# A fused attention and max-out kernel on one core: the written-out order of its work is replaced, and its dummy products get wider

## The chip, the core and the metric

The kernel runs on one NeuronCore of a Trainium2 chip. Five engines take their instructions from queues of their own, each strictly in the order in which they were written: TensorE (PE in the profile; its weight loads are listed as PEld), VectorE (DVE), ScalarE (ACT), GpSimd (POOL) and SyncE (SP), which here only issues DMAs. An instruction waits at the head of its queue until the semaphores that it needs are up, and everything behind it waits with it. The metric is the device time of one execution in microseconds (us).

## The reference, cut to what matters

Four batches of eight heads, 768 positions, head size 64. Three of the heads see all earlier keys; the other five see the first four keys and a window of 64. The concatenated heads are the input of a max-out layer.

```
scores = q @ k.T / 8                                # per head, 768 x 768
mask   = causal                                     # is_retrieval heads (0, 2, 6)
mask   = causal & (key < 4 | query - key < 64)      # the others
a      = softmax(scores masked)
x      = concat over heads of a @ v                 # 3072 tokens x 512
g      = maximum(x @ w1, x @ w2)                    # 512 -> 1024, twice
out    = g @ w_out                                  # 1024 -> 512
```

## The kernel before, in words

The kernel computes the layer as relu(x (w1 - w2)) w_out + x (w2 w_out): so it needs the difference w12 = w1 - w2 (line 1139, "sub"), and once the product w2o = w2 w_out on PE (lines 1156 and 1183).

Work is cut in eight halves: four batches, 384 query rows each. The order of the halves is batch 0 first half, batch 1 first half, batch 0 second half, batch 1 second half, then the two halves of batch 2 and of batch 3. A half goes through these steps. q, k and v land as f32 in one of three staging slots (tile ld). They are cast to bf16 (qb, vb; lines 366 and 368 are the helper that copies, on ACT and on DVE or POOL). PE turns q and k (line 645; in the last three halves a DMA does), a copy takes them out of PSUM (qk). PE makes the scores (915), ACT takes their exponential (930, tile at), DVE multiplies with the mask (955), PE forms the weighted sums (980), DVE divides by the row sums (997 and 1007, "norms") into x. x is turned (1103 on PE for the first three halves, by DMA for the others) and the layer follows one half later: "up" (1206, 32 products of 384 columns), relu on ACT (1231) or DVE (1233), "down" (1263, 36 products of 512 columns), a copy to ot, a store (1291).

Batch 0's first half has a detour for v: it is loaded in the layout that DMA moves best, and PE spreads it to the right rows (688).

The weights come through the same three slots. w2 comes in two column halves of 1 MB, w1 likewise, w_out in four pieces of 0.5 MB. Each w2 half is cast (w2b, four casts of 1024 columns in all), turned by PE in four groups of eight (1156), taken out of PSUM as w2t. Each w_out piece is cast to wob. The four pieces of w_out feed four groups of products for w2o (1183): group c needs w2t c and wob c. Slots are freed by casts: w_out's first piece may be issued when the q of batch 0's first half is cast, the second when q and k are, the third when k is, the fourth when v is; batch 1's q and k go into the slot of w_out and wait for the casts of wob.

What stands in front of all this: the order is not found by a scheduler at run time. The kernel collects 1097 operations, and `Order.run` (line 137 on) emits them in the order of a table of tokens, PLAN, and a short one, LAST. A token is the operation's number, a letter for the engine that does it (p PE, a ACT, v DVE, g POOL, s SP) and the PSUM banks that it takes; so the table sets three things: the order on each engine's queue, which engine does a cast or copy that several could do, and the bank. A token x is a dummy product on PE (line 353): `warmer`, a tile of zeros, times itself, into a bank that is free, its result never read. The dummies fill places where PE would have nothing to do in the first 24 us.

## Time and profile before

| what | value |
|---|---|
| median of 3 runs (lowest, highest) | 176.43 us (176.25, 176.6) |
| the profiled execution: first to last instruction | 175.4 us |
| PE busy | 168.5 us, 96% |
| ACT busy | 126.3 us, 72% |
| DVE busy | 122.0 us, 70% |
| POOL busy | 34.2 us, 19% |
| granted TensorE clock, mean | 0.997 |
| DMA | 36.14 MB, mean 206 GB/s; 334 to 389 GB/s in the page's slices from 4.4 to 26 us |

The profiled execution's own span is 175.4 us; the median of the runs lies 1.03 us above it. Times in the profile are us from the first instruction of that execution. A row of the timeline gives start, length, engine, line, operation, what it writes and reads, how many equal instructions were merged, and in brackets how long the engine had been idle before and what released it. The records of PE products overlap, since a product's record runs until its result has left the array: a row with 8 products of 512 columns is 1.89 us long, and the next product may start some 0.16 us before its end.

### The profile page before, as it was taken

The numbers are of one execution on the slowest core, as the hardware profiler recorded it, in microseconds if no ns is written. First come the engines' busy times: TensorE is split into PE (matmuls) and PEld (weight loads), VectorE is DVE, ScalarE is ACT, GpSimd is POOL, SyncE is SP. The second block draws the span as 40 slices with busy tenths as digits, with TensorE's granted clock in tenths as the row PEclk, the third lists the DMA queues.
The fourth block names the chain that finished last, engine by engine and source line by source line (L and its number), as shares of the span: only waits on it lengthen the run. The fifth ranks groups of instructions, "written<-read, shape, count | busy, mean of one in ns | idle before, by whom it ended". The sixth has DMA issues, their size and how long they took to land.

```text
span 175.4 us, 4945 instructions
## 1 busy us (share of the span) xinstructions
PE 168.5 (96%) x1795; PEld 105.5 (60%) x1816; DVE 122.0 (70%) x331; ACT 126.3 (72%) x280; POOL 34.2 (19%) x78
## 2 busy tenths in 40 slices
PE   7999799999999999999999999999999999999993
PEld 7976575655665666666656545764565566545542
DVE  5579899686999997887858666666884168941211
ACT  3499807998999998999997669795858598405200
POOL 5732132422414613040200240000012000000000
PEclk9999999999999999999999999999999999999998
DMA  4999999999899999992597993339999334453004
GB/s 129 334 371 389 387 382 333 214 312 298 201 248 258 281 300 211 234 283 71 152 190 192 238 225 76 71 69 237 213 242 176 67 87 153 154 153 122 0 7 179
DMA packets 77661, 36.14 MB, mean 206 GB/s; under 512 B 59202, under 2 KB 72514, under 8 KB 77634
## 3 DMA queue, kind: packets, MB, share of 16 engines
q1 hardware_dynamic: 77488, 35.73, 78.4%
q8 instruction: 15, 0.25, 0.6%
q14 instruction: 12, 0.10, 0.2%
q10 hardware_dynamic: 146, 0.07, 0.1%
HBM read 25.17 MB, written 6.29 MB: 179 GB/s over the span
## 4 chain that ended last, share of the span: by engine, by line
PE 85%; DMA 6%; POOL 3%; issue 2%; DVE 2%; POOLq 0%; ACT 0%; DVEq 0%; SPq 0%; ACTq 0%
PE ps L1263 36%; PE ps L1206 24%; PE ps L915 9%; PE ps L980 8%; DMA ld<-in_moe_w_dram 6%; PE ps L645 3%; PE ps L1183 3%; POOL tab L1605 1%; PE ps L1103 1%; DVE at L955 1%; PE ps L353 1%; DVE x L1007 0%; POOL tab L1619 0%; POOL g L705 0%; POOLq L1670 0%
## 5 line engine op out<-in xcount | busy, mean ns | idle before, releaser
L930 ACT ACTIVATE at<-ps 128x512 bf16<-128x512 f32 (+2 forms) x134 | 64.1, 573 | 6.4 <-PE ps L915 6.2
L1206 PE MATMUL ps<-xt,w 128*128 128x384 bf16 x256 | 45.8, 326 | 0.0
L1263 PE MATMUL ps<-wob,g 128*128 128x512 bf16 (+2 forms) x192 | 44.7, 370 | 0.4
L955 DVE TENSOR_TENSOR at<-at,tab 128x1024 bf16<-128x1024 bf16 (+5 forms) x56 | 29.9, 549 | 10.7 <-ACT at L930 10.3
L1206 PEld LDWEIGHTS <-w 128*128 128x128 bf16 x256 | 23.9, 98 | 16.0 <-issue 0.4
L1263 PEld LDWEIGHTS <-g 128*128 128x128 bf16 x200 | 18.0, 98 | 18.8 <-issue 0.2
L1231 ACT ACTIVATE g<-ps 128x384 bf16<-128x384 f32 x37 | 18.0, 502 | 11.1 <-PE ps L1206 10.0
L1233 DVE TENSOR_SCALAR g<-ps 128x384 bf16<-128x384 f32 x27 | 14.6, 550 | 15.8 <-PE ps L1206 15.7
L1263 PE MATMUL ps<-w2o,xt 128*128 128x512 bf16 (+2 forms) x90 | 23.5, 370 | 0.5
L1007 DVE TENSOR_TENSOR x<-ps,rez 128x192 f32 x64 | 22.7, 355 | 1.6
L368 POOL CAST qb<-ld 128x384 bf16 (+1 forms) x28 | 13.2, 505 | 50.5 <-DMA ld<-in_q_dram 30.6
L366 ACT COPY ot<-ps 128x512 f32<-128x512 f32 (+1 forms) x18 | 10.4, 575 | 17.0 <-PE ps L1263 16.8
L980 PEld LDWEIGHTS <-at 128*128 128x128 bf16 x477 | 18.6, 97 | 6.3 <-DVE at L955 1.2
L980 PE MATMUL ps<-vb,at 128*128 128x65 bf16 x387 | 20.4, 193 | 0.4 <-DVE at L955 0.4
L915 PE MATMUL ps<-qk 64*128 64x128 bf16 (+1 forms) x330 | 18.4, 228 | 0.2
L915 PEld LDWEIGHTS <-qk 64*128 64x128 bf16 x330 | 12.2, 94 | 7.2 <-issue 4.7
L368 DVE COPY qk<-ps 128x384 bf16<-128x384 bf16 (+1 forms) x17 | 11.3, 693 | 3.9 <-PE ps L645 3.8
L1263 PEld LDWEIGHTS <-xt 128*128 128x128 bf16 x100 | 8.9, 97 | 8.5
L366 ACT CAST qb<-ld 128x384 bf16 (+1 forms) x31 | 11.8, 440 | 2.8 <-DMA ld<-in_q_dram 1.7
L353 PE MATMUL ps<-warmer 128*128 128x128 bf16 x133 | 12.1, 256 | 1.4 <-POOL warmer L1655 1.2
L353 PEld LDWEIGHTS <-warmer 128*128 128x128 bf16 x133 | 10.5, 118 | 1.7 <-POOL warmer L1655 1.2
L368 POOL CAST vb<-ld 128x192 bf16 x15 | 5.7, 406 | 24.6 <-DMA ld<-in_v_dram 24.5
(74 smaller groups left out, 161.4 us busy)
## 6 DMA issues: line engine op xcount, KB each, us to landing
ld<-in_v_dram SPq DMA_DIRECT2D x21, 256.0 KB, 5.0
ld<-in_moe_w_dram SPq DMA_DIRECT2D x4, 1024.0 KB, 11.8
out_dram<-ot SPq DMA_DIRECT2D x16, 256.0 KB, 3.4
ld<-in_q_dram SPq DMA_DIRECT2D x5, 768.0 KB, 7.3
ld<-in_k_dram SPq DMA_DIRECT2D x5, 768.0 KB, 8.4
ld<-in_k_dram SPq DMA_DIRECT2D x9, 256.0 KB, 4.5
ld<-in_q_dram SPq DMA_DIRECT2D x9, 256.0 KB, 4.9
ld<-in_moe_w_out_dram SPq DMA_DIRECT2D x4, 512.0 KB, 10.6
```

Source lines behind the costliest of these rows:

```text
L353: nc.tensor.matmul(banks[e][:, 0:128 * m].rearrange("p (m c) -> p m c", m=m), lhsT=warm, rhs=warm.unsqueeze(1).to_broadcast([128, m, 128]) ...
L366: nc.scalar.copy(out=out, in_=in_)
L368: eng[e].tensor_copy(out=out, in_=in_)
L915: nc.tensor.matmul(to.rearrange("p (i c) -> p i c", c=128), lhsT=lhsT, rhs=q_of(n, i, m)[rows], start=True, stop=True, skip_group_check=True,)
L930: nc.scalar.activation(out=at[:, bk, 0:w], in_=bank(("ps", b, hf, t), part=bk)[:, 0:w], func=ACT.Exp, scale=scale,)
L955: eng[e].tensor_tensor(out=at, in0=at, in1=tbl, op=ALU.mult)
L980: nc.tensor.matmul(po[:, hh, i - NT * hf, :], lhsT=ats[:, T["at", b, hf, t] % NAT, bk, e * 128:(e + 1) * 128], rhs=rhs, start=first, stop= ...
L1007: nc.vector.tensor_tensor(out=xs[:, HALVES.index((b, hf)) % NX, :, bass.ds(heads[2 * p + hh], 1), :], in0=po[:, hh, :, 0:D].unsqueeze(2), ...
L1206: nc.tensor.matmul(bank(key)[:, 0:HALF], lhsT=w[:, kc, fc * 128:(fc + 1) * 128], rhs=xts[:, HALVES.index((b, hf)) % NXT, :, kc, :], start= ...
L1231: nc.scalar.activation(out=g, in_=ph, func=ACT.Relu)
L1233: nc.vector.tensor_scalar_max(out=g, in0=ph, scalar1=0.0)
L1263: nc.tensor.matmul(bank(key)[:, cols], lhsT=lhsT, rhs=(w2o if kind == "x" else wob)[:, c, cols], start=(e == 0), stop=(e == len(steps) - 1),)
```

## The change

The two tables are replaced by new ones with the same 1097 operations; what each operation computes, and its buffers, are untouched. The numbers of operations by engine shift, since a few casts and copies are given to another engine: tokens for ACT go from 279 to 265, for DVE from 305 to 314, for POOL from 62 to 67. A new token y is a dummy product of 512 columns (the `dummy` function had that size as an argument already). There are 29 of these in place of 133 of 128 columns. As `run` loses no line and the table has two lines fewer, every line below it is numbered two lower in the changed kernel (1183 becomes 1181).

```diff
@@ -137,10 +137,10 @@ Order.run
         for token in plan.split():
-            if token[0] == "x":
+            if token[0] in "xy":
                 spot, _, times = token[1:].partition("*")
                 for _ in range(int(times or 1)):
-                    self.dummy(int(spot))
+                    self.dummy(int(spot), 4 if token[0] == "y" else 1)
                 continue
@@ -152,64 +152,62 @@
 PLAN = """
-0s x0*3 1s x0*5 2s x0*36 3s 66a 50v x0*3 28a 64v x0 48g x0 58a x0 68p0 26a 25g x1*2 52p1 56a 69v 44p2 x3 4s
...
+0s y0 1s y0 2s y0 y1*3 y2*3 3s y3*3 y4 56a 26v y4 50a 58v y4 64a 66v y5 28a 48v y5 8s 52p0 44p1 60p2 4s y3 45v
...
 LAST = """
-1082v 1085p 1083s 1077a 1086p 1078s 1089p5 1087v 1090p 1091p 1088s 1092a 1093a
+1082a 1083s 1084p6 1077v 1085p 1078s 1086p 1089p5 1087a 1090p 1091p 1088s 1092v 1093a
 """
```

Three places of the new order are shown. The names carry the program's buffer numbers: ld is the staging slot, w2b the cast of w2, w2t its turned form, wob the cast of w_out, vb the spread v, at the exponentials, rez the reciprocals of the row sums, x the attention's result.

SP, the first loads. Before, from batch 0's q to batch 1's k:

```order
L426 DMA ld_61<-in_q_dram 128x8x192
L426 DMA ld_61<-in_k_dram 128x8x192
L426 DMA ld_61<-in_v_dram 128x8x192
L531 DMA ld_61<-in_moe_w2_dram 128x4x512
L552 DMA ld_61<-in_moe_w_out_dram 128x2x512
L531 DMA ld_61<-in_moe_w2_dram 128x4x512
L552 DMA ld_61<-in_moe_w_out_dram 128x2x512 x2
L531 DMA ld_61<-in_moe_w1_dram 128x4x512
L552 DMA ld_61<-in_moe_w_out_dram 128x2x512
L531 DMA ld_61<-in_moe_w1_dram 128x4x512
L426 DMA ld_61<-in_q_dram 128x8x192
L426 DMA ld_61<-in_k_dram 128x8x192
```

and now:

```order
L424 DMA ld_61<-in_q_dram 128x8x192
L424 DMA ld_61<-in_k_dram 128x8x192
L424 DMA ld_61<-in_v_dram 128x8x192
L529 DMA ld_61<-in_moe_w2_dram 128x4x512 x2
L550 DMA ld_61<-in_moe_w_out_dram 128x2x512 x4
L529 DMA ld_61<-in_moe_w1_dram 128x4x512 x2
L424 DMA ld_61<-in_q_dram 128x8x192
L424 DMA ld_61<-in_k_dram 128x8x192
```

The second half of w2 goes ahead of all of w_out, and w1 behind all of it; the four pieces of w_out come in their own order.

ACT, from the last copy of v to the first products of the layer. Before:

```order
L366 CAST vb_143<-ps0_155 128x8x64
L930 ACTIVATE at_148<-ps4_159 128x512
L366 COPY w2t_140<-ps7_162 128x1024
L930 ACTIVATE at_148<-ps2_157 128x512
L366 CAST w2b_138<-ld_61 128x4x256
L930 ACTIVATE at_148<-ps3_158 128x512
L366 COPY w2t_140<-ps5_160 128x1024
L366 COPY w2t_140<-ps2_157 128x1024
L366 COPY xt_150<-ps2_157 128x1024
L366 COPY xt_150<-ps1_156 128x512
```

and now:

```order
L364 CAST w2b_138<-ld_61 128x4x256
L364 CAST vb_143<-ps2_157 128x8x64
L928 ACTIVATE at_148<-ps4_159 128x512
L928 ACTIVATE at_148<-ps5_160 128x512
L928 ACTIVATE at_148<-ps7_162 128x512
L364 CAST wob_142<-ld_61 128x1024
L364 COPY w2t_140<-ps0_155 128x1024
L364 CAST wob_142<-ld_61 128x1024
L364 COPY xt_150<-ps3_158 128x1024
L364 COPY xt_150<-ps6_161 128x512
```

Two casts of w_out (its second and third piece) stand in ACT's queue, two copies of w2t have left it. Of the four casts of w_out POOL had three and DVE one; now ACT has two, DVE one (the first piece) and POOL one (the last).

DVE, from the last cast of w2 to the first norms. Before:

```order
L368 COPY w2t_140<-ps5_160 128x1024
L997 RECIPROCAL rez_63<-ps1_156 128x6
L368 CAST w2b_138<-ld_61 128x4x256
L1007 ISA
L1007 TENSOR_TENSOR x_149<-ps1_156,rez_63 128x3x64
```

and now:

```order
L366 CAST w2b_138<-ld_61 128x4x256
L366 COPY w2t_140<-ps6_161 128x1024
L366 CAST wob_142<-ld_61 128x1024
L953 TENSOR_TENSOR at_148<-at_148,tab_60 128x1024
L366 COPY w2t_140<-ps1_156 128x1024
L366 COPY w2t_140<-ps3_158 128x1024
L953 TENSOR_TENSOR at_148<-at_148,tab_60 128x1024
L995 RECIPROCAL rez_63<-ps2_157 128x6
```

The norms of batch 0's first half, which began among the masks and casts, all stand behind them now, and the four subs behind the norms as before.

On PE the last dummies stood behind the last weighted sums of batch 0's first half (29 of 128 columns, ahead of the second group of products for w2o); now the last dummy stands ahead of the third turned group of w2, and from there on PE has real work alone. The layer's eight "up" of the first half now come in one row, ahead of the turning of batch 1's q, and two groups of "down" stand among the turnings.

More of the change, by code (lines that the diff above doesn't have):

```diff
@@ new lines @@
+144p 117p3 119p6 118a 155p 148p 121v 150p 120a 146p 151a 125v 211p2 19s 156a 209p0 213p3 129v 215p6 133v 18s
+222p4 216a 214a 220p7 223a 157v 181g 195a 226p6 197a 212v 183g 210a 224p3 159g 169a 227v 167g 221a 17s 163p4
+149a 187p2 225v 201p0 173p6 147v 218p7 20s 158a 160g 170a 198g 184v 182a 165p1 21s 229p 174v 168g 166a 196g 164v
+202a 175p3 425s 188a 189p5 203p6 176v 190a 244p10 240p42 177v 246a 179v 219p3 204v 171g 242a 172g 200v 241a 185g
+247p50 205v 245a 252p62 186a 191v 423s 230p 207v 180a 199v 254a 193v 161v 249a 208v 234p 243v 253a 248a 206v
@@ new lines @@
+294g 337v 433a 295g 334p2 339v 300g 443g 333a 330p7 335v 451g 438p3 314v 331a 316v 396p6 306v 326v 397p 439a
+398p 426s 380p14 372p05 440v 381a 305v 392p27 315v 399p 373a 233s 342p3 400v 393a 554s 446p1 374a 343v 349p0
+673s 320a 375v 382a 317v 325g 350p 307a 447v 581a 562g 676s 394a 571g 402v 384p25 493p34 401v 385a 377p17 453g
+561v 386a 327v 388p62 376v 675s 351p 390a 383v 395v 379a 565p5 448v 389a 344p2 378a 391v 352a 403p7 387v 454p6
+353s 410p1 455a 404p 405p 236s 415p 409p0 566a 416v 411p 572v 345p 551s 418v 495a 417v 671s 406v 346p 456v 553s
@@ new lines @@
+841s 776a 718p0 711a 615a 720p3 933s 719v 772a 358s 716p5 704v 769v 814a 929s 771a 781p 712p4 758v 842s 688v
+721v 607p7 713a 693g 833v 777v 927s 791p0 722p6 815s 938v 608p 952v 723a 782v 765v 835v 816s 773v 724p1 709v
+714p3 953v 725a 784v 488s 726p4 715a 821s 793p 785p6 794v 792p1 717v 797p 786p 931s 787p 736p3 928s 788v 783v
+930s 823v 790v 727p 789v 798v 799v 796v 728p 800v 825v 843v 845v 795v 609p 729v 801s 737p 610a 882p52 616s
+894p61 884a 885p04 896a 611s 902p72 738p 937g 886a 730s 945g 883a 944g 904a 731p1 826g 887a 942g 895a 732p 960g
@@ new lines @@
+959g 903a 897v 951a 898p05 939g 890p24 878p67 891a 733p 905v 879a 936v 892a 949v 941s 943v 868p2 880a 957v 893v
+958a 734v 849p6 900a 940s 888v 899a 881v 859p4 950a 857p7 955s 916p1 858a 918p 861p5 919v 850a 860v 947s 961a
+847p0 901v 862a 906p7 921v 855p6 920v 621s 956v 889v 907p 853p4 856v 735s 908v 851p5 910v 954s 854a 848a 917p1
+922p 739a 911p6 923v 912p 925v 863p4 946s 852a 913v 914v 924v 864p 948v 909v 965v 915v 1001p03 926s 997p51 1002a
+1007p76 869p 998a 1008a 962s 870p 999a 1009a 865p 1003a 740s 871a 1010p05 963s 866v 1022p71 1012a 1015p63
```

84 lines of the change are left out of this document (31 added, 53 removed).

## The prediction

> **What bounds the kernel now.** I read the head of the page and the chain of waits first, then PE's own waits.
>
> ```profile
> span 175.4 us, 4945 instructions
> PE 168.5 (96%) x1795; PEld 105.5 (60%) x1816; DVE 122.0 (70%) x331; ACT 126.3 (72%) x280; POOL 34.2 (19%) x78
> PE 85%; DMA 6%; POOL 3%; issue 2%; DVE 2%; POOLq 0%; ACT 0%; DVEq 0%; SPq 0%; ACTq 0%
> L353 PE MATMUL ps<-warmer 128*128 128x128 bf16 x133 | 12.1, 256 | 1.4 <-POOL warmer L1655 1.2 <-ACT at L930 0.2
> PE ps L1156 <- DVE w2b L368: 0.8, 1, 0.8
> PE ps L980 <- DVE at L955: 0.4, 2, 0.2
> ```
>
> PE is 85% of the chain. Its only named waits are 1.2 us before the first dummy and 1.4 us after it, all before 22 us. But 12.1 us of its busy time are dummies, so its free time is there. PE's timeline shows where:
>
> ```profile
> 13.76 2.10 PE L688 MATMUL ps<-xt,g 128*128 128x512 bf16 x8
> 16.65 0.78 PE L980 MATMUL ps<-vb,at 128*128 128x65 bf16 x20
> 17.44 1.25 PE L1183 MATMUL ps<-wob,w2t 128*128 128x512 bf16 x5
> 19.48 1.07 PE L1156 MATMUL ps<-tab,w2b 128*128 128x128 bf16 x16 [0.78 <-DVE w2b L368]
> 21.65 0.54 PE L980 MATMUL ps<-vb,at 128*128 128x65 bf16 x12 [0.15 <-DVE at L955]
> 22.13 1.78 PE L353 MATMUL ps<-warmer 128*128 128x128 bf16 x29
> 23.75 1.89 PE L1183 MATMUL ps<-wob,w2t 128*128 128x512 bf16 x7
> 30.25 2.76 PE L1206 MATMUL ps<-xt,w 128*128 128x384 bf16 x16
> 32.85 0.67 PE L645 MATMUL ps<-tab,qb 128*128 128x128 bf16 x9
> 36.24 0.62 PE L915 MATMUL ps<-qk 64*128 64x128 bf16 x15
> ```
>
> The reader is to see two places where PE lacks work after 19 us: it waits 0.78 us for the second half of w2, and at 22.13 it turns dummies for 1.62 us until w_out is there. From 23.75 on it goes from one real product to the next. So the span is: the time until PE has unbroken work, the work behind that, and some 3 us of tail. Only the first of these can move much. Later stretches show little that is idle:
>
> ```profile
> 35.00:60.00 25.00, 24.59 (x267) 15.10 (x268) 22.19 (x61) 23.59 (x56) 9.85 (x20) 1.00 1.03 266
> 60.00:95.00 35.00, 34.64 (x462) 22.25 (x467) 27.54 (x77) 33.14 (x75) 5.29 (x11) 1.00 0.87 208
> 95.00:160.00 65.00, 64.48 (x621) 36.83 (x628) 41.48 (x120) 43.28 (x97) 5.27 (x13) 1.00 0.69 150
> ```
>
> (columns: window, length, PE, PEld, DVE, ACT, POOL busy, clock, DMA share, GB/s.) PE is idle for 0.41, 0.36 and 0.52 us there. ACT is the second bound up to 95 us: 56.7 of 60 us busy.
>
> **The change part by part.** *The landings.* These set when PE has real work:
>
> ```profile
> 7.72 0.47 SPq L531 DMA_DIRECT2D ld<-in_moe_w_dram  x1
> 9.45 0.88 SPq L552 DMA_DIRECT2D ld<-in_moe_w_out_dram  x2
> 13.38 0.70 DVE L368 CAST w2b<-ld 128x1024 bf16<-128x1024 f32 x1 [0.42 <-DMA ld<-in_moe_w_dram]
> 16.04 1.04 POOL L368 CAST wob<-ld 128x1024 bf16<-128x1024 f32 x1 [3.82 <-DMA ld<-in_moe_w_out_dram]
> 18.73 0.69 DVE L368 CAST w2b<-ld 128x1024 bf16<-128x1024 f32 x1 [0.66 <-DMA ld<-in_moe_w_dram]
> 21.45 1.04 POOL L368 CAST wob<-ld 128x1024 bf16<-128x1024 f32 x1 [4.37 <-DMA ld<-in_moe_w_out_dram]
> 25.46 1.94 POOL L368 CAST wob<-ld 128x1024 bf16<-128x1024 f32 x1 [2.96 <-DMA ld<-in_moe_w_out_dram]
> ```
>
> Between 18.73 and 21.45 two pieces of w_out land (0.5 MB each), between 21.45 and 25.46 half of w1 and a piece: 2 and 3 units of 0.5 MB, so 1.35 us a unit. In the new order w2's second half (issued at 7.72 before) has one unit less ahead of it: 18.73 - 1.35 = 17.4. From below it is bounded by the place of the piece that stood there, 16.04; from above by no move, 18.73. Of the three I take 17.4, by the unit. The pieces of w_out follow: the first at 18.7 (as many bytes ahead of it as w2's half had), then 20.1, 21.4, 22.8; w1's halves at 25.5 and 28.2.
>
> *From there to the layer.* PE's last dummy ends near 17.3: before it stand v's spread (at 13.7, since the last cast of v still follows four exponentials on ACT, as it did at 13.76), two turned groups of w2 and two of the scores. The third turned group starts at 17.4 + 0.7 (the cast) = 18.1. What PE has to do from there to the end of the first half's "up" is counted from the rows. Before, from 19.48 to 36.24 it is 16.76 us; less the dummies (23.75 - 22.13 = 1.62) and the wait (0.15) it is 14.99. 24 turnings of q and k (9 of them take 0.67 - 0.16 = 0.51, so 1.36 in all) now come later: 13.63. Behind 18.1 now come also the 20 weighted sums of 16.65 (0.79 to the next row) and the first three groups for w2o (six products; eight take 1.89 - 0.16 in the row of 23.75, which lacks one, so 1.30): 15.72. So "up" would end at 33.8 if nothing waits; in the old order the same work is done at 36.24 - 1.36 = 34.9. That is a gain of 1.1.
>
> *What it costs in waits.* The new order hangs more on ACT and DVE here:
>
> ```profile
> 11.97 3.54 ACT L930 ACTIVATE at<-ps 128x512 bf16<-128x512 f32 x7
> 15.33 0.65 ACT L366 CAST vb<-ps 128x512 bf16<-128x512 f32 x1
> 20.16 1.92 ACT L366 COPY w2t<-ps 128x1024 bf16<-128x1024 bf16 x2
> 23.83 1.53 DVE L1007 TENSOR_TENSOR x<-ps,rez 128x192 f32 x4
> L1139 DVE TENSOR_TENSOR w<-ld x4: 1209/1213/2059, 25.3 to 29.5; 128x1024 bf16<-128x1024 f32 x4
> ```
>
> An exponential takes (15.33 - 11.97) / 7 = 0.48 on ACT, a copy of 1024 columns 0.95; so the next instruction starts some 0.1 before a record's end, and DVE's casts count 0.6. ACT: w2's cast from 17.4 to 18.35, v's copy 18.8, three exponentials 20.3, the second piece of w_out 21.3 (landed 20.1), w2t 22.2, the third piece 23.2. PE reaches the products that need these pieces at 21.8 and 24.1: 0.4 and 0.9 us of slack. DVE: w2 18.0, w2t 18.6, first piece of w_out 19.4, a mask, two w2t and a mask at 0.6 each 21.8, then a wait of about a microsecond for the weighted sums, eight norms at 0.385 and four reciprocals: 26.5. PE asks for x at 26.25, a wait of 0.3. The subs follow at 1.15 each, 27.7 to 31.1, PE's pairs of "up" need them at 29.0, 30.3, 31.6, 32.9: covered. If that cover goes, each microsecond by which DVE is late is one microsecond of PE. POOL casts one piece of w_out in place of three, and the rows in which a cast on POOL runs beside DVE (2.06 for a sub, 1.2 without) can come once. So 1.1 - 0.3 = 0.8 is left, between -0.3 (landing at 18.73) and 1.1 (PE not before 17.3 and no wait; less than the 1.9 that the landing at 16.04 would give, since DVE's norms do not follow).
>
> *Batch 1's first half.* Its q and k landed at 30.70 and 33.07, with as many bytes ahead of them in the new order:
>
> ```profile
> 22.52 0.37 SPq L426 DMA_DIRECT2D ld<-in_q_dram  x1
> 23.07 1.38 SPq L426 DMA_DIRECT2D ld<-in_k_dram  x1
> 30.70 0.64 POOL L368 CAST qb<-ld 128x192 bf16 x2 [3.30 <-DMA ld<-in_q_dram]
> 33.07 1.52 POOL L368 CAST qb<-ld 128x192 bf16 x5 [1.73 <-DMA ld<-in_k_dram]
> ```
>
> They wait for casts of w_out, done at 21.3 and 23.2 in the new order, against issues at 22.52 and 23.07: ten microseconds ahead of the landing, and not later by more than 0.2. PE, done with "up" at 34.1, turns q, has a "down" to 35.6, and turns k: covered by 0.9 us and more.
>
> *Dummies.* The first ones and the cast that hides them:
>
> ```profile
> 1.16 5.51 PE L353 MATMUL ps<-warmer 128*128 128x128 bf16 x50 [1.16 <-POOL warmer L1655]
> 8.28 1.11 ACT L366 CAST qb<-ld 128x192 bf16 x4 [1.03 <-DMA ld<-in_k_dram]
> ```
>
> 17 of 512 columns at the start take about 17 x 4 x 0.106 = 7.2 us at the pace of the first ones (50 of 128 columns in 5.51) and end near 8; the turnings of q start a microsecond later than before, hidden behind k, whose casts start at 8.28. They cost nothing.
>
> *The rest.* ACT loses 14 of 279 operations, about 6 us of work; up to 95 us it was busy for 56.7 of 60. PE's idle 0.8 us up to 95 could go with that, or stay: I take 0.3. From below: other queues of SP, other casts on DVE, up to 0.5 us more idle than before, as much as the later stretch shows. *The tail* keeps its products; the last copy moves from ACT to DVE, where 128 columns cost less than the 384 of the row below, so at most 0.3 more: nothing.
>
> ```profile
> 171.76 0.56 DVE L368 COPY ot<-ps 128x384 f32<-128x384 f32 x1 [1.42 <-PE ps L1263]
> 172.47 0.27 ACT L366 COPY ot<-ps 128x128 f32<-128x128 f32 x1 [1.31 <-PE ps L1263]
> ```
>
> Sum: 175.4 - 0.8 - 0.3 = 174.3 for the profiled execution; the runs' median was 1.03 above its span, so 175.3.
>
> ```profile
> L1183 PE MATMUL ps<-wob,w2t 128*128 128x512 bf16 x30 | 7.6, 379 | 0.1
> ```
>
> The row of w2o's products gives a record 379 ns, while 7 of them (of 8) took 1.89 - 0.16 above, a pace of 216: a busy PE need not be a full one. The Trainium skill says in "Trainium Kernel Development and Optimization" (Performance Expectations) that matmul busy time tells badly how much room a kernel has, since matmuls are pipelined. The trace agrees, by these two numbers. By that rule PE's 96% hides room in every stretch and the gain could be several times my 0.3; that is the fast rival below.
>
> **The rivals.** *A (forecast): the front keeps most of what it gains.* 175.3.
> *B: more room than the idle rows show.* PE's real products sum to about 153 us at their paces (276 of 512 columns at 0.216, 256 of 384 at 0.163 and so on); from 36.24 to the last copy at 172.5 about 131 of these take 136. If ACT's relief returns a third of these 5 us: 173.6. For it: ACT's 33.14 of 35; against it: PE waits for no one there by name.
> *C: ACT and DVE eat the gain.* The front's norms are late by another half microsecond and batch 1's first exponentials start 0.7 us later than before, with ACT 94% busy behind them: 176.3, within the bound.
> *D: slower. ACT's queue blocks on w_out.* The second and third piece are cast by ACT, and ACT waits for their landing with everything behind it: w2t, both copies of xt, w2o, the first relus. The pieces are issued when batch 0's q and k are cast, and one cast of k now stands behind two copies on ACT (near 10.9; SP issued two pieces at 9.45 before). From 0.4 us late on it decides; two units late (2.7 us) is 2.3 us on PE: 176.4 - 0.8 + 2.3 = 177.9 with nothing else gained. Against it: the queue still holds 2 MB at 11 us.
>
> **How the numbers follow.** A 0.47, B 0.13, C 0.20, D 0.20. I take 0.2% (0.35 us) as what the measurement tells from no change. A is faster but for its lower edge (0.44), B faster, C same for the most part (0.14, slower 0.06), D slower: faster 0.58, same 0.17, slower 0.25. The range from 173.6 (B) to 177.0 leaves out half of D and little else. A's own range is 174.6 to 176.0.
>
> **What would show it.** Right: no dummy after 18 us and the third turned group near 18.1; "up" done near 34; PE's first product of x near 26.5. The step on landings falls if w2's second cast starts at 18.7, D shows as a wait of ACT on in_moe_w_out over a microsecond, C as waits of PE on DVE (x) near 26 or on ACT (at) from 37 to 60. PE idle in 35 to 95 above 1.5 us would make the prediction wrong as a whole.

## The result

The changed kernel took 181.2 us in the median of four runs (180.76 to 182.48), against 176.34 (176.25 to 176.6) for the kernel before: a ratio of 1.0287, with an interval from 1.0249 to 1.0325. It is slower by 4.9 us. The prediction said 175.3, with a range from 173.6 to 177.0.

The head of the page of the changed kernel, its chain of waits by engine and by line, and the row of the dummies:

```profile
span 179.1 us, 4731 instructions
PE 169.0 (94%) x1692; PEld 98.4 (55%) x1712; DVE 119.3 (67%) x340; ACT 120.3 (67%) x266; POOL 32.8 (18%) x83
PE 52%; DMA 22%; DVE 8%; SPq 7%; ACT 6%; issue 3%; DVEq 0%; another core or an unknown queue 0%
L351 PE MATMUL ps<-warmer 128*128 128x512 bf16 x29 | 9.4, 478 | 1.2 <-POOL warmer L1653 1.2
```

The span of the profiled execution is 3.7 us longer. That is less than the 4.9 us between the medians: in every execution with both on record the time is 1.66 to 1.86 us above the span, so the 1.03 us between the median and the profiled span of the kernel before is no such offset. Its profiled execution was by that some 0.7 us slower than its median (its executions beside the experiments have spans of 174.3 to 175.9, 174.75 in the median). Whatever is compared below with its one profile looks better by about that much at the end. ACT is busy for 6.0 us less, as the change meant it. The chain is the first sign of where to look: PE made up 85% of it before and makes up 52% now, and DMA went from 6% to 22%, with 7% for SP's queue.

**The front did what was predicted, and more.** PE's timeline of the changed kernel, from the third turned group of w2 to the end of the first half's "up":

```profile
16.74 1.07 PE L1154 MATMUL ps<-tab,w2b 128*128 128x128 bf16 x16
17.64 0.77 PE L978 MATMUL ps<-vb,at 128*128 128x65 bf16 x20
18.94 0.39 PE L1181 MATMUL ps<-wob,w2t 128*128 128x512 bf16 x1 [0.53 <-DVE wob L366]
...
25.42 0.84 PE L1101 MATMUL ps<-tab,x 128*128 128x128 bf16 x12 [0.35 <-DVE x L1005]
...
33.02 0.83 PE L643 MATMUL ps<-tab,qb 128*128 128x128 bf16 x12
```

"Up" is done at 33.0, where the prediction had 33.8 to 34.1, and the wait for x is 0.35 against a predicted 0.3.

**The loss is behind 95 us.** The windows of the kernel before and then of the changed one (columns: window, length, busy time of PE, PEld, DVE, ACT, POOL, granted clock, DMA share, GB/s):

```profile
95.00:120.00 25.00, 24.88 (x242) 14.58 (x243) 17.67 (x54) 18.03 (x42) 2.96 (x8) 1.00 0.65 144
120.00:145.00 25.00, 24.76 (x245) 14.18 (x247) 14.50 (x38) 18.69 (x42) 2.31 (x5) 1.00 0.88 165
```

```profile
35.00:75.00 40.00, 39.27 (x466) 24.52 (x470) 32.48 (x94) 37.16 (x82) 10.20 (x25) 1.00 1.08 257
75.00:95.00 20.00, 19.89 (x258) 12.78 (x259) 16.43 (x50) 18.38 (x44) 5.38 (x12) 1.00 0.75 167
95.00:120.00 25.00, 23.12 (x235) 13.33 (x236) 15.23 (x49) 16.18 (x38) 3.55 (x6) 1.00 0.82 171
120.00:145.00 25.00, 23.09 (x214) 12.26 (x215) 13.58 (x39) 16.29 (x38) 3.13 (x8) 1.00 0.71 172
```

PE is idle for 1.88 + 1.91 = 3.79 us from 95 to 145, against 0.12 + 0.24 = 0.36 before. DVE and ACT are not the bound there by their busy time, 58% and 65% of it; and yet they are what PE waits for.

To see gains and losses by time, I use one measure throughout: the **lead**. It is the real work on PE that a kernel has begun by a time t (each kind of product counted at its usual pace, 0.216 us for 512 columns, 0.162 for 384 and so on, scaled for records that are missing) less what the kernel before had begun by then. A constant lead means that the two kernels run alike; where it falls, this one loses. It is worked out from all of PE's records and is good to some 0.4 us.

```
lead in us at    35     90     95    100    110    120    130    140   later
changed        +1.7   +1.3   +1.2   +0.3   -0.1   -1.2   -2.2   -3.8   -3.7
```

The front's 1.7 us are there at 35 and 1.3 of them still at 90. The sixteen other kernels below that have this front whole show +1.1 to +1.9 at 35. Part of the 1.3 is probably the one profile that all is compared with: e2 below, which keeps the old order up to 83 us, reads +0.5 at 80 without any change. From 95 to 140 5.0 us are lost, 3.4 of them as idle time in the windows above and the rest as products that follow one another less closely.

**What the engines stood for.** The rows of DVE and of ACT in the changed kernel, from 60 to 141 us, whose idle time a landing ended and which cost over half a microsecond; and the same of the kernel before, whose only one on DVE this is (kx is a copy of a part of the turned k):

```profile
97.20 0.22 DVE L366 COPY kx<-qk 64x192 bf16<-64x192 bf16 x1 [0.94 <-DMA qk<-qb]
115.13 0.61 DVE L366 CAST vb<-ld 128x192 bf16 x2 [3.15 <-DMA ld<-in_v_dram]
122.29 0.69 DVE L366 COPY ot<-ps 128x512 f32<-128x512 f32 x1 [0.54 <-DMA out_dram<-ot]
127.24 0.36 DVE L366 CAST qb<-ld 128x384 bf16 x1 [0.59 <-DMA ld<-in_k_dram]
127.60 0.51 ACT L364 CAST qb<-ld 128x384 bf16 x1 [1.73 <-DMA ld<-in_k_dram]
135.38 0.23 DVE L366 COPY kx<-qk 128x192 bf16<-128x192 bf16 x1 [1.70 <-DMA qk<-qb]
```

```profile
134.69 0.87 DVE L368 CAST vb<-ld 128x192 bf16 x3 [0.88 <-DMA ld<-in_v_dram]
```

In its five rows DVE stands 6.9 us for landings, ahead of masks, norms and copies that are ready. PE's timeline of the changed kernel has these waits from 95 to 145:

```profile
98.70 0.20 PE L978 MATMUL ps<-vb,at 128*128 128x65 bf16 x1 [0.34 <-DVE at L953]
107.16 2.77 PE L1204 MATMUL ps<-xt,w 128*128 128x384 bf16 x16 [0.39 <-DMA xt<-x]
116.77 0.20 PE L978 MATMUL ps<-vb,at 128*128 128x65 bf16 x1 [0.85 <-DVE at L953]
123.03 0.23 PE L913 MATMUL ps<-qk 64*128 64x128 bf16 x2 [0.15 <-DVE ot L366]
128.46 1.04 PE L1261 MATMUL ps<-w2o,xt 128*128 128x512 bf16 x4 [0.60 <-DMA xt<-x]
136.45 0.31 PE L978 MATMUL ps<-vb,at 128*128 128x65 bf16 x5 [0.78 <-DVE g L1231]
139.65 0.32 PE L913 MATMUL ps<-qk 64*128 64x384 bf16 x1 [0.27 <-DVE x L1005]
```

They sum to 3.4 us: 2.4 for what DVE does late, 1.0 for two turnings of x (xt), which stand in SP's queue too. The row of 1.70 at 135.38 is behind PE's wait of 0.78, the row of 3.15 at 115.13 behind its 0.85. Not every such wait costs PE: DVE stands 1.89 us more for a turning at 145.99, and no wait of PE follows.

**Where the landings come from.** SP's queue of the kernel before, and that of the changed kernel, in the same stretch:

```profile
104.14 13.15 SPq L668 DMA_TRANSPOSE qk<-qb  x9
117.39 0.52 SPq L1291 DMA_DIRECT2D out_dram<-ot  x1
```

```profile
104.95 2.22 SPq L666 DMA_TRANSPOSE qk<-qb  x1
107.21 0.58 SPq L437 DMA_DIRECT2D ld<-in_v_dram  x1
107.84 3.90 SPq L666 DMA_TRANSPOSE qk<-qb  x3
111.78 0.58 SPq L437 DMA_DIRECT2D ld<-in_v_dram  x1
...
116.02 2.82 SPq L666 DMA_TRANSPOSE qk<-qb  x2
```

The kernel before issued the nine turnings of q and k for the next half in one row; the new order puts loads and stores between them. The view of DMA issues (count, median us from issue to landing) has the turnings of the kernel before, and then of the changed one:

```profile
qk<-qb SPq DMA_TRANSPOSE x24, 2.4
```

```profile
qk<-qb SPq DMA_TRANSPOSE x24, 3.2
```

Taken one by one between 104 and 120 us, five of the eight turnings of the kernel before that have a record land 2.3 to 2.4 us after their issue, the other three 3.0 to 4.0. In the changed kernel those right behind a load or a store land 3.1 to 5.3 us after their issue (the one issued at 116.02 landed at 121.34), 0.4 to 1.9 us after the load or store ahead of them, and the one that follows a turning 2.3. The Trainium skill says in "DMA: Bandwidth & Descriptors" (Queues, rings and completion order) that a transfer's semaphore lands only after every earlier write of the same DMA engine, across its queues. The rows agree with that: a short turning behind a load reports no earlier than the load. No run here separates this reason from others.

### The profile page after: what moved, and what is told of

Same layout as the page of the kernel before. It is cut to its first block, busy times and chain, and to the rows that moved or that the text cites. A ratio compares the mean times of both kernels' runs of the same rounds, so it can differ in the third digit from the quotient of the medians.

```text
span 179.1 us, 4731 instructions
## 1 busy us (share of the span) xinstructions
PE 169.0 (94%) x1692; PEld 98.4 (55%) x1712; DVE 119.3 (67%) x340; ACT 120.3 (67%) x266; POOL 32.8 (18%) x83
## 4 chain that ended last, share of the span: by engine, by line
PE 52%; DMA 22%; DVE 8%; SPq 7%; ACT 6%; issue 3%; DVEq 0%; another core or an unknown queue 0%
PE ps L1261 20%; PE ps L1204 16%; DMA ld<-in_moe_w_out_dram 6%; DMA xt<-x 6%; PE ps L913 5%; PE ps L978 5%; DMA ld<-in_k_dram 5%; DVE x L1005 4%; DMA qk<-qb 4%; ACT at L928 3%; PE ps L1181 2%; PE ps L643 2%; SPq L529 2%; DMA ld<-in_v_dram 2%; DVE at L953 2%
## 5 line engine op out<-in xcount | busy, mean ns | idle before, releaser
L928 ACT ACTIVATE at<-ps 128x512 bf16<-128x512 f32 (+2 forms) x134 | 65.5, 574 | 8.6 <-PE ps L913 8.3
L953 DVE TENSOR_TENSOR at<-at,tab 128x1024 bf16<-128x1024 bf16 (+5 forms) x56 | 28.2, 519 | 8.6 <-ACT at L928 8.3
L1261 PEld LDWEIGHTS <-g 128*128 128x128 bf16 x200 | 18.2, 98 | 20.2 <-issue 0.8
L1005 DVE TENSOR_TENSOR x<-ps,rez 128x192 f32 x64 | 22.8, 356 | 1.7
L366 POOL CAST qb<-ld 128x384 bf16 (+1 forms) x32 | 14.5, 481 | 47.4 <-DMA ld<-in_k_dram 26.2
L978 PE MATMUL ps<-vb,at 128*128 128x65 bf16 x387 | 20.1, 193 | 2.2 <-DVE at L953 1.2
L913 PE MATMUL ps<-qk 64*128 64x128 bf16 (+1 forms) x330 | 19.7, 228 | 0.5 <-DVE x L1005 0.3
L366 DVE COPY ot<-ps 128x512 f32<-128x512 f32 (+1 forms) x12 | 7.8, 653 | 11.7 <-PE ps L1261 7.8
L364 ACT COPY ot<-ps 128x512 f32<-128x512 f32 (+1 forms) x13 | 7.7, 592 | 11.6 <-PE ps L1261 11.4
L364 ACT CAST qb<-ld 128x192 bf16 (+1 forms) x26 | 10.5, 450 | 4.7 <-DMA ld<-in_k_dram 3.0
L366 POOL CAST vb<-ld 128x192 bf16 x22 | 7.6, 367 | 26.6 <-DMA ld<-in_v_dram 22.7
L366 DVE COPY kx<-qk 128x192 bf16<-128x192 bf16 (+5 forms) x33 | 7.2, 235 | 5.4 <-DMA qk<-qb 4.5
L351 PE MATMUL ps<-warmer 128*128 128x512 bf16 x29 | 9.4, 478 | 1.2 <-POOL warmer L1653 1.2
```

The lines of the kernel that those rows point to most:

```text
L351: nc.tensor.matmul(banks[e][:, 0:128 * m].rearrange("p (m c) -> p m c", m=m), lhsT=warm, rhs=warm.unsqueeze(1).to_broadcast([128, m, 128]) ...
L364: nc.scalar.copy(out=out, in_=in_)
L366: eng[e].tensor_copy(out=out, in_=in_)
L913: nc.tensor.matmul(to.rearrange("p (i c) -> p i c", c=128), lhsT=lhsT, rhs=q_of(n, i, m)[rows], start=True, stop=True, skip_group_check=True,)
L928: nc.scalar.activation(out=at[:, bk, 0:w], in_=bank(("ps", b, hf, t), part=bk)[:, 0:w], func=ACT.Exp, scale=scale,)
L953: eng[e].tensor_tensor(out=at, in0=at, in1=tbl, op=ALU.mult)
```

## The experiments

The theory after this comparison: the front's gain is real, and the order from 75 us on loses it and more, since DVE and ACT stand in their queues for landings from SP's queue. Against it stood three rivals: that nothing gained in the front can carry to the end, since the landings behind it come at times of their own; that the wide dummies cost something; and that one single wait (the cast of v at 115) is the whole loss.

All kernels compute the reference in full. Where the old and the new table are joined, both parts have the same operations, each once; the joined kernels have only the dummies of their first part. Every run is compared with the kernel before, on the same chip.

### Which stretch loses: the two orders joined

The table follows the one order up to a seam and the other behind it. e1 goes from the new to the old at 84.5 us, e2 from the old to the new at the same operation, near 83; e16 leaves the new order at about 36 us, e17 at about 74.

```diff
 e1   ... 540p3   (new up to here)
+ 804s 806s 702a 686g 695v ...      (old from here)
 e2   ... 540p3   (old up to here)
+ 573g 677s 583v 808s ...           (new from here)
 e16  ... 217p0   (new up to here)
+ 24s 262a 426s 263v 238a 239s ...  (old from here)
 e17  ... 470p3   (new up to here)
+ 239s 437g 457g 441v 449a 807s ... (old from here)
```

> The changed kernel's tables up to operation 540 (a weighting product of batch 1, second half; TensorE reaches it at about 84.5 us of the changed kernel), and from there all operations still left in the order and on the engines of the kernel before. Theory 1 (the loss lies in the order after 90 us: SP's queue and what stands behind its landings on DVE): the products done by 90 us are 1.2 us ahead of the kernel before, and the old order keeps that: 176.4 - 1.2, about 175.2 us, at most 176. Theory 2 (the lead of the first half is borrowed: casts and copies put off there come due later): 179 to 181 us. Theory 3 (the later half is bound by its landings at fixed times, no lead carries through): 176.4 us.

> The reverse: the kernel before up to operation 540, with its narrow dummies, and from there all that is left in the changed kernel's order and on its engines. Theory 1: the new order's loss after 90 us (about 5 us against the kernel before) without its lead of 1.2 us: 181 to 182.5 us. Theory 2: 176 to 177 us. Theory 3 (the later half is bound at fixed times by SP): 181.2 us, as the changed kernel.

> The changed kernel's tables up to operation 217 (the first output product of batch 0, which TensorE reaches at about 36 us), with its dummy products, and from there all that is left in the order and on the engines of the kernel before (whose own later dummies are left out); at this place the two orders have done the same operations but for twelve, where the place of e1 had 34 and its seam cost 5.5 us, 3.1 of them one wait. Theory (the front gains 1.7 us by 35 us, the order after 90 loses): the gain stays to the end, 174.7 to 175.3 us, faster than both kernels. Rival (the front's gain is borrowed, or the later part is bound by landings at fixed times): 176.2 to 177 us or more.

> The same with the place at operation 470 (an up product of batch 0's second half, about 74 us), where 24 operations differ, none of them a transpose on SP. Theory: the lead there was 0.8 to 1.1 us, and the loss comes later: 175.3 to 176 us. Rival (the new order of 36 to 74 us is what the later part suffers from): 177.5 us or more.

| kernel | median us (range) | ratio (interval) | span |
|---|---|---|---|
| e1, new then old at 84.5 | 182.11 (181.71 to 182.76) | 1.0318 (1.0284 to 1.0352) | 180.3 |
| e2, old then new at 83 | 180.06 (179.35 to 181.77) | 1.0223 (1.0158 to 1.0287) | 177.9 |
| e16, new then old at 36 | 178.59 (178.14 to 179.34) | 1.0108 (1.0078 to 1.0139) | 177.2 |
| e17, new then old at 74 | 177.79 (177.69 to 178.24) | 1.0071 (1.0046 to 1.0096) | 176.0 |

```
lead in us at    40    65    75    80    90    95   100   120   140   later
e1                                     +0.9  -2.7  -5.1  -4.8  -4.9   -4.9
e2                                +0.5             -0.6  -1.9  -2.4
e16            +1.6   (-2.0 at 60)  then -1.2 to -1.9 throughout
e17                  +1.4  +0.8  -0.5   then -0.25 to -0.6 throughout
```

None of the four came out in the range that the theory gave; e16 and e17 lie in those of their rivals. What speaks for the theory is in the traces.

e2 has none of the new front, and loses 2.9 us between 80 and 140: 1.8 of them behind 100, where its seam is past. So the new order of that stretch loses without anything from the front. e17 has the new front and middle and the old rest. It gets back 3.4 of the 4.9 us; from 95 us on PE shows no idle time in fifty microseconds:

```profile
75.00:95.00 20.00, 18.50 (x253) 11.47 (x251) 14.28 (x45) 18.28 (x42) 3.38 (x8) 1.00 0.91 194
95.00:120.00 25.00, 25.00 (x245) 14.64 (x244) 17.83 (x54) 18.65 (x44) 2.32 (x6) 1.00 0.60 133
120.00:145.00 25.00, 25.00 (x248) 14.17 (x247) 14.29 (x38) 17.97 (x42) 2.31 (x5) 1.00 0.83 168
```

What e17 loses, it loses at its seam, where the two orders don't fit: one wait, in PE's timeline,

```profile
77.37 1.46 PE L1205 MATMUL ps<-xt,w 128*128 128x384 bf16 x8 [1.50 <-ACT at L929]
```

turns a lead of 0.8 into a lag. e16 loses 1.6 us at its seam near 45 and about two more up to 60. Behind both seams the difference stays as it is for a hundred microseconds: no fixed times of landings pull it back to zero. But what stays there is a lag. That the front's lead would stay as well is argued from this and not shown, and that part of it is borrowed (work that the new order puts off and that comes due at the seam) is not excluded. That a clean seam would have shown a gain at the end was not run.

e1 was meant to answer the same and did not, since its seam broke worse. DVE's row and PE's, and two windows behind them:

```profile
93.29 0.23 DVE L367 COPY kx<-qk 128x192 bf16<-128x192 bf16 x1 [5.69 <-DMA qk<-qb]
94.72 0.40 PE L914 MATMUL ps<-qk 64*128 64x128 bf16 x8 [3.10 <-DVE x L1006]
```

```profile
96.00:98.00 2.00, 1.67 (x9) 0.76 (x7) 1.71 (x5) 0.89 (x4) 0.00 (x0) 0.52 1.07 142
98.00:100.00 2.00, 1.92 (x7) 0.94 (x7) 0.81 (x2) 0.88 (x2) 0.00 (x0) 0.63 0.60 175
```

It is the theory's mechanism at its plainest: a copy of 0.23 us stands 5.69 us for a turning, norms that are ready stand behind it, and PE stands 3.10 us for the norms. Then PE runs at a granted clock of 0.52 to 0.63 for four microseconds. From 100 us on the lead is constant here too.

### The dummies

Each dummy of 512 columns becomes four of 128, everything else as in the changed kernel.

```diff
-y1*3
+x1*12
```

> The changed kernel with each of its 29 dummy products of 512 columns written as four of 128 at the same place (116 in all); order and everything else as changed. If the dummies' width is free, as predicted: 181.2 us within 0.5. If the wide dummies hold the clock or the queue and make part of the loss: 179 to 180.5 us. If the narrow ones cost more of TensorE's time: over 181.8 us.

182.6 us (182.54 to 183.44), ratio 1.0363 (1.0332 to 1.0394). The wide dummies are not the loss: with narrow ones the kernel is 1.4 us slower still, as in the third case of the expectation. But PE's time in the front is not the reason. The lead is +1.3 at 35 us, within what the kernels with the wide ones show, and +0.5 at 105. Then it falls to -2.9 at 120: DVE, with the same order as in the changed kernel, stands 2.06 us for a turning at 113.44 and 3.03 us for v at 117.32, and PE 2.89 us for a mask at 118.96, where it stood 0.85 in the changed kernel. So one and the same order loses more or less, as its landings fall; why they fall otherwise here is open.

### Waits on DVE and ACT

e3 moves the three casts of v, for which DVE stands at 115, behind what PE needs next; nothing else. e9 moves the same three further, behind the last cast of q and k, on top of e5 (next section), so it has SP's row of nine turnings too. e13 is e12 (the section after that) with two casts of v on ACT about ten places back. DVE's queue in e3, and ACT's in e13:

```diff
 e3, DVE
 L953 TENSOR_TENSOR at<-at,tab 128x1024
-L366 COPY vb<-ld 128x3x64      (three of them, among masks and copies)
 L995 RECIPROCAL rez<-ps_157 128x6
 ...
+L366 COPY vb<-ld 128x3x64      (three)
 L366 COPY ot<-ps_159 128x512
 e13, ACT
-L364 COPY vb<-ld 128x3x64      (two)
 L928 ACTIVATE at<-ps_155 128x512
 ...
 L928 ACTIVATE at<-ps_155 128x512
+L364 COPY vb<-ld 128x3x64      (two)
```

> The changed kernel with three casts of v of the last half (vb<-ld, operations 938, 952, 953) moved behind the last normalisation of batch 2, second half, in DVE's order; nothing else. In the changed kernel DVE stood from 111.98 to 115.13 us before the first of them, for a load that landed at 115.10. Theory 1 (in-order engines stand behind landings): masks and normalisations come up to 3.1 us earlier, TensorE's wait of 0.85 us at 116.77 goes; SP gets to the transpose of x only at 123.40 all the same, so no more than 0.5 to 1.5 us come back: 179.7 to 180.7 us. Rival (DVE's wait is hidden, TensorE's order or the clock makes the loss): 181.0 to 181.4 us.

> The kernel e5_turns_run with the three casts of v put still further back on DVE: behind the copy out of PSUM (ot<-ps) and two masks, which in e5 stood 3.42 us behind them for loads that landed at 123.7 us. In e5 TensorE was 0.76 us ahead of the kernel before at 120 us and 3.4 us behind at 125. Theory (the transposes in one run keep the lead; DVE standing for a landing ahead of a copy that frees a bank lost it): the 3.4 to 4.2 us lost there come back, 177.5 to 179.5 us. Rival (the scores of batch 3 wait for the landings themselves, not for DVE): still above 182 us.

> The kernel e12_six_early_run, in which nothing was lost after 105 us (TensorE stays 2.3 to 2.8 us behind the kernel before from there to 140) and 3.6 us were lost between 90 and 95, with two casts of v of batch 3 (vb<-ld, operations 820 and 839) put 7 to 11 places back on ACT, behind the exponentials of batch 2. In e12 ACT stood 3.93 us before the first of them, for a load that landed at 91.0 us in place of 85.0. Theory (what decides is an engine in order that stands for a landing in front of work that is ready; all such places have to go): 2 to 3.6 us come back, and with the lead of 1 us 175.5 to 177.5 us. Rival (the loss only moves to the next landing, whatever is mended): 180.5 to 182.5 us.

e3: 181.98 us (181.1 to 183.24), ratio 1.0328 (1.027 to 1.0386), no better than the changed kernel. The wait at 115 is gone, and the windows tell where the time went:

```profile
95.00:120.00 25.00, 24.27 (x247) 14.00 (x250) 16.08 (x50) 16.38 (x38) 3.55 (x6) 1.00 0.79 176
120.00:145.00 25.00, 21.79 (x207) 11.62 (x208) 13.32 (x39) 16.02 (x37) 3.13 (x8) 1.00 0.70 174
```

PE has 1.15 us more in the first window and 1.30 less in the second. So the rival of the single wait falls.

e9: 186.84 us (186.22 to 187.72), ratio 1.0608 (1.056 to 1.0655). The casts free the staging slots, and the loads of q and k now wait for them: DVE's row

```profile
131.04 0.36 DVE L366 CAST qb<-ld 128x384 bf16 x1 [5.67 <-DMA ld<-in_k_dram]
```

is what came of it, and PE waits 6.3 us for an xt.

e13: 180.84 us (178.82 to 181.41), ratio 1.0272 (1.025 to 1.0294), against 181.62 and 1.0314 for e12. The wait that it was made for goes, and at 95 us the lead is -0.3 where e12 has -2.1. But PE now waits 1.09 us for an xt at 93.06 and 1.06 us for a mask at 100.99, and from 110 us on the two are within 0.8 us of each other: the loss moved on, as the rival said.

### SP's order, with e3's casts

Four kernels make rows of turnings again, all with e3's casts: e4 a row of six after the loads, e5 a row of nine ahead of them, e6 as e5 with two copies of DVE (kx) moved behind the norms of batch 3's first half and the six turnings there in one row, e7 as e6 with rows for the half before too. SP's queue in e5:

```diff
-L666 DMA_TRANSPOSE qk<-qb 128x3x128 x4
+L666 DMA_TRANSPOSE qk<-qb 128x3x128 x3
 L1120 DMA_TRANSPOSE xt<-x 128x12x128
+L666 DMA_TRANSPOSE qk<-qb 128x3x128 x9
+L1289 DMA out_dram<-ot 128x512 x2
 L437 DMA ld<-in_v_dram 128x8x64
 L437 DMA ld<-in_k_dram 128x8x64
-L666 DMA_TRANSPOSE qk<-qb 128x3x128       (nine turnings in all among
-L437 DMA ld<-in_v_dram 128x8x64           loads and stores)
 ...
+L437 DMA ld<-in_v_dram 128x8x64 x2
+L437 DMA ld<-in_q_dram 128x8x64 x2
```

> As the kernel with the casts moved, and SP's order from 100 to 126 us of the changed kernel made anew: the transpose of x of batch 2, first half, ahead of one of q and k; the eight loads of the last half in one run behind two transposes, then the other six transposes of q and k in one run, then the transpose of x of the second half, then two stores. Operations and all other engines stay. Theory 1: x of the first half lands 1.3 us earlier, the load that DVE stood for some 3 us earlier, x of the second half at about 123 in place of 128.4: 2 to 3.5 us come back, 177.7 to 179.2 us. Rival (SP's order makes no difference since the transfers take their time anyway): 179.7 us or what the casts alone give.

> The changed kernel with the three casts of v moved as in the run before, and SP's order from 100 to 126 us turned the other way round: the transpose of x first, then all nine transposes of q and k in one run, then two stores, then the eight loads of the last half in one run, then the transpose of x of the second half. Theory (the copies kx<-qk on DVE and the scores on TensorE stand for landings of qk<-qb; a run of transposes lands 2.35 us after each issue, one behind a load or store 3.2 to 5.3): the last of these lands near 116 us in place of 122.6, the waits of TensorE from 107 to 129 go, 2 to 3 us come back: 178 to 179 us. Rival (the loads of the last half are what is late, the transposes have room): the loads land 3 to 9 us later than in the changed kernel for five of the eight, and the kernel is slower than 182.

> The kernel before this one, and also the copies of k of the last half (kx<-qk, operations 956 and 948), for which DVE stood 1.7 us at 133.7 to 135.4 in the changed kernel, put behind the normalisations of batch 3's first half, and the six transposes of q and k there put in one run with two stores behind them. Theory: another 1 to 1.5 us come back, 176.5 to 178 us. Rival (the wait only moves to the next landing): as the kernel before this one within 0.5 us.

> The kernel before this one, and also SP's order from 78 to 100 us made in runs: four transposes of q and k of batch 2's second half, three loads, the transpose of x, four transposes, five loads, two stores. In the changed kernel DVE stood 0.94 us at 97.2 for a transpose that was issued behind two loads, and TensorE's lead fell from 1.2 to 0.3 us between 95 and 100. Theory: about 1 us more comes back, 175.3 to 177 us, which is the lead of 1.2 us kept to the end at the best. Rival (the loads put behind them are needed first): slower than the kernel before this one.

| kernel | median us (range) | ratio (interval) | longest waits of PE, us |
|---|---|---|---|
| e4 | 190.17 (189.83 to 190.75) | 1.0773 (1.0741 to 1.0805) | 5.0 for qk, 3.9 for a copy of ot |
| e5 | 185.24 (182.81 to 186.07) | 1.0518 (1.049 to 1.0546) | 3.9 for a copy of ot |
| e6 | 184.17 (183.71 to 184.9) | 1.0428 (1.0403 to 1.0453) | 4.6 for a copy of ot |
| e7 | 192.26 (191.38 to 192.8) | 1.0879 (1.0838 to 1.0919) | 4.7 for x, 3.2 for qk, 2.2 for ot |

All are worse, each by a new wait that can be named, and by the lower clock that follows it (last section). e5 is the most telling: the median landing of a turning is 2.4 us again, and the lead is kept up to 120 us (+0.76, where the changed kernel has -1.2). But the loads of v now come behind nine turnings, and DVE stands for v ahead of the copy that frees a bank for PE:

```profile
123.72 0.87 DVE L366 CAST vb<-ld 128x192 bf16 x3 [3.42 <-DMA ld<-in_v_dram]
```

So the time of a landing is not the loss by itself. It is the landing against the place of the operation that waits for it. e4 shows again what a long stall does to the clock; PE's row and two windows:

```profile
125.68 0.50 PE L913 MATMUL ps<-qk 64*128 64x128 bf16 x6 [5.01 <-DMA qk<-qb]
```

```profile
125.00:130.00 5.00, 1.08 (x13) 0.69 (x14) 0.74 (x3) 0.28 (x1) 0.80 (x2) 0.50 0.76 218
130.00:135.00 5.00, 3.81 (x18) 1.68 (x19) 1.75 (x4) 3.88 (x10) 0.00 (x0) 0.50 0.37 144
```

### Loads issued earlier, and rows of turnings

e10 issues six loads of q and k of the last half at 71 us instead of among the turnings; e11 adds e9's casts to that; e12 adds the row of nine turnings. e14 is e12 with other loads moved forward, in the order in which they are needed: four of batch 3's first half go to 72 us, and four of the six of the last half into the places that they leave; e15 is e14 with e13's casts; e18 is e14 with DVE and ACT relieved near 95 (a kx behind a mask, three casts of v from ACT to POOL, one turning issued two loads earlier). SP's queue in e14, whose casts on DVE stand as in e9:

```diff
 L1289 DMA out_dram<-ot 128x512
+L437 DMA ld<-in_k_dram 128x8x64
+L437 DMA ld<-in_q_dram 128x8x64
+L437 DMA ld<-in_k_dram 128x8x64
+L437 DMA ld<-in_q_dram 128x8x64
 L437 DMA ld<-in_v_dram 128x8x64 x2
...
-L666 DMA_TRANSPOSE qk<-qb 128x3x128 x4
+L666 DMA_TRANSPOSE qk<-qb 128x3x128 x3
 L1120 DMA_TRANSPOSE xt<-x 128x12x128
...
+L666 DMA_TRANSPOSE qk<-qb 128x3x128 x9
+L1289 DMA out_dram<-ot 128x512 x2
 L437 DMA ld<-in_q_dram 128x8x64
 L437 DMA ld<-in_k_dram 128x8x64
+L437 DMA ld<-in_v_dram 128x8x64 x3
 L1120 DMA_TRANSPOSE xt<-x 128x12x128
```

> The changed kernel with one thing moved: the six loads of q and k of the last half, which SP issues between 104 and 123 us among the transposes, issued together behind the store at 71.4 us, where SP has nothing to issue until 76.6 us (their slots are read out by 71.84 us). Theory (from 94 to 137 us SP's one queue is full, and each load among transposes delays the next landing): SP is 3.6 us further ahead from 104 on, x of batch 2's second half lands 2 to 4 us earlier than 128.4, DVE's wait at 112 to 115 is 1 us shorter, the last transposes come earlier: 178 to 179.7 us. Rival (SP's queue has room, and the loss is in the order of the engines): 181 to 182 us. Second rival (the loads fill the queue ahead of batch 2's transposes at 78 us): slower.

> The six loads early as in e10, and the three casts of v put back on DVE as in e9. Theory: DVE no longer stands at 112 to 115 us and SP is not late for x: 176.5 to 178.5 us. Rival (DVE's wait and SP's load are hidden behind something else): as e10 within 0.5.

> As e11, and the nine transposes of q and k from 100 to 122 us in one run ahead of two stores and the three loads of v, x of the first half ahead of them. Theory: the last of them lands near 116 us, no wait of TensorE above 0.5 us is left from 100 to 130 us: 175.5 to 177.5 us. Rival (the loads of v are what is late): the loads land near 120.5 us and DVE stands for them near 127: slower than e11.

> The changed kernel with the three casts of v put back on DVE as in e11 and SP's order from 72 to 123 us made so: four loads of q and k of batch 3's first half, whose slots were read out at 53 us, in the idle time at 72.5 to 76.6; in the places they leave, four of the six loads of the last half; the nine transposes at 100 to 116 in one run, with x ahead of them; the other five loads behind. [...] Theory: no stretch loses: 175.3 to 177 us. Rival (the loss moves on): 180 to 182 us.

> e14 with the two casts of v put back on ACT as in e13. Theory: as e14 or up to 1 us faster, 175 to 176.5 us. Rival: as e14, 180 to 182 us.

> e14_loads_swapped, whose one remaining loss lies at 90 to 105 us (TensorE from 1.33 us ahead to 0.18 behind), with three things more: the transpose that DVE stood 0.90 us for at 97.5 issued two loads earlier on SP, DVE's copy of it (kx<-qk, operation 692) behind a mask, and three casts of v taken from ACT, which was busy 18.4 of the 20 us from 90 to 110, to POOL, which was idle. Theory: 0.5 to 1.2 us come back, 178.3 to 179 us. Rival (the loss moves on): as e14, 179.5 us or more.

| kernel | median us (range) | ratio (interval) | span | lead at 90, 100, 120, 140 |
|---|---|---|---|---|
| e10 | 182.46 (180.88 to 182.72) | 1.0321 (1.0261 to 1.0382) | 180.7 | +1.6, -3.7, not read, -4.4 |
| e11 | 182.18 (181.24 to 183.07) | 1.0341 (1.0281 to 1.0401) | 179.8 | +1.1, -3.6, -3.6, -3.6 |
| e12 | 181.62 (180.29 to 182.48) | 1.0314 (1.0281 to 1.0348) | 178.6 | +1.1, -2.4, -2.5, -2.6 |
| e14 | 179.48 (178.16 to 179.94) | 1.0181 (1.0153 to 1.0209) | 176.4 | +1.3, +0.2, +0.1, -1.3 |
| e15 | 179.96 (178.82 to 180.32) | 1.0188 (1.0143 to 1.0233) | 178.1 | not read, -0.8, -1.0, -2.5 |
| e18 | 179.9 (178.92 to 180.85) | 1.0162 (1.0119 to 1.0204) | 179.1 | +1.1, +0.2, -2.6, -2.6 |

With the six loads early, casts and turnings rearranged (e11, e12), little or nothing is lost behind 100 us any more; but 3.5 to 4.7 us go between 90 and 100, where the loads of v now come later than the casts that stand for them on ACT:

```profile
91.08 0.60 ACT L364 CAST vb<-ld 128x192 bf16 x2 [3.93 <-DMA ld<-in_v_dram]
```

In e11 part of that is the clock: 1.3 us of its lead go between 95 and 100, where the clock is down to 0.50 for two microseconds (last section). In e12, whose waits before 95 are as long and whose clock stays at 1.00, 0.2 go there. So the step from e11 to e12 does not show what the row of turnings is worth.

e14 avoids the wait of 3.93 with its four loads. Its windows and its row of SP's queue:

```profile
95.00:120.00 25.00, 24.23 (x248) 14.19 (x251) 16.05 (x51) 16.50 (x38) 3.56 (x6) 1.00 0.58 143
120.00:145.00 25.00, 24.09 (x235) 13.14 (x236) 14.92 (x43) 18.15 (x41) 3.14 (x8) 1.00 0.66 172
```

```profile
102.97 12.44 SPq L666 DMA_TRANSPOSE qk<-qb  x9
```

PE's idle time from 95 to 145 goes from 3.79 to 1.68 us, and the kernel is 1.7 us faster than the changed one in the median and 2.7 in the profiled span. Of DVE's five rows above that stood for a landing one is left, the first, at 0.90. The casts alone (e3), the six loads alone (e10) and these two together (e11) were no better than the changed kernel, and the casts with the row of turnings (e4, e5, e9) slower; casts, turnings and e14's loads together give the only gain over the changed kernel that an edit of the new table showed clear of its interval. e15 and e18 add nothing: e18's relief near 95 brings a new wait of 1.7 us of PE for a turning, and its lead falls from +0.2 to -2.4 between 100 and 110.

No version is faster than the kernel before.

## Why the prediction was wrong, step by step

**The front: right in mechanism, too small.** The landings of w_out and w1 that an engine stood for came within 0.5 us of what was put (18.2, 19.8, 22.6 and 28.1 against 18.7, 20.1, 22.8 and 28.2), and the wait for x held. The landing of w2's second half did not: it came at 16.0, two units earlier than before and not one, so the third turned group starts at 16.74 and not at 18.1. Its lower bound, the landing at 16.04 with a cast of 0.7 behind it, was the better one. The term 0.8 measured 1.7 at 35 us, beyond its own bound of 1.1, which had DVE's norms not follow: they did, PE's first product of x is at 25.42 where 26.25 was put.

**Batch 1's q and k, and the dummies: right.** PE turns q from 33.02 on without a wait. The first 17 dummies end at 7.3, near 8 as predicted, and e8 shows that the narrow form would have been no better.

**ACT's relief: wrong by a little.** ACT lost 6.0 us of work as worked out, and from 35 to 95 PE was idle for 0.73 + 0.11 = 0.84 us as against 0.77 before: 0.3 us were expected and none came. The lead even falls by 0.4 there. The larger return of rival B, a third of 5 us, did not come either.

**The step that failed** is the sentence under *The rest*, "From below: other queues of SP, other casts on DVE, up to 0.5 us more idle than before, as much as the later stretch shows". It took a stretch in which PE was idle for 0.52 of 65 us as one that has nothing to lose: "Only the first of these can move much. Later stretches show little that is idle." But little idle time says that this order fits, not that another one will. The term put at 0.5 us at most measured 3.4 us more idle (3.79 against 0.36 from 95 to 145), and 5.0 us of lead. The order of SP's queue there could have been read beforehand: nine turnings in a row (104.14) against the same turnings among loads, with DVE's casts of v ahead of masks.

**The sign that was named was in the wrong place.** "PE idle in 35 to 95 above 1.5 us would make the prediction wrong as a whole": it was 0.84, and the prediction was wrong as a whole.

**The rivals.** None of the three was it. D, the slow one, had the right mechanism (an engine's queue blocks on a landing) in the wrong place: ACT stood 0.83 us for w_out in the front, and PE did not wait for it there; DVE and ACT on v, k and the turnings behind 95 are where the time went. C's half microsecond at batch 1's first exponentials did not come either.

**What is shown of the cause, and what is not.** Shown: the loss lies in the new order behind about 75 us (e2, e17); 3.4 of its 5.0 us are waits of PE for late work of DVE and late turnings of x, and DVE's own long waits there are for landings (the rows above; e1 and e5 show such a wait handed on at its plainest); and ordering turnings, loads and casts with one another gives back 1.7 us of the median (e14). Open: the 1.7 us by which e14 is still slower than e17; the 1.6 us of the loss that no wait of PE names; whether the front's lead would last to the end; and which of e14's three parts does how much, since no kernel with one or two of them (e3, e5, e9, e10, e11) was faster than the changed one. e14's lead falls by about 1 us between 90 and 105, where ACT's queue is full (18.4 of 20 us busy from 90 to 110 in the changed kernel, 19.1 in e14), and by 1.4 between 120 and 140; the one try at the first (e18) moved the loss and did not remove it.

## What to carry to other kernels

An order that is planned on landings measured under the old order can change those landings; so read the queue of the engine that issues DMAs, and each in-order queue behind it, in every stretch that is reordered, above all where nothing is idle now. The sign to look for is an operation that waits for a landing and stands ahead of work that is ready: its price is that of everything behind it, as far as another engine needs that soon. Here such waits could not be mended one by one, since what was moved forward put something else back: e3 mended one place, e4 to e7 and e9 two or more, and all gave back what they won, or more.
